# A fused attention and low-rank mixer kernel on one core: the fifth batch's k and q turned in two halves around the first mixer's u, casts moved by some heads, and the first batch's V placed later

## The chip, the cores and the metric

The kernel runs on one core of one Trainium2 chip. A core has TensorE (PE: matmuls and transposes into PSUM banks), VectorE (DVE), ScalarE (ACT), GpSimd (POOL) and SyncE (SP), each with a queue of its own that is worked off in order, and 16 DMA engines that all queues share. The metric is the device time of one execution in microseconds; the median of several runs is given. "Before" is the kernel without the change.

## The reference

Eight batches of eight heads, 576 tokens, head width 64, model width 512, inner width 2048:

```python
scores = scale * np.matmul(q, k.transpose(0, 1, 3, 2))
cum = np.cumsum(np.maximum(s, 0.0), axis=-1)
bias = -(cum[:, :, :, None] - cum[:, :, None, :])
scores = np.where(causal, -1000000000.0, scores + np.minimum(bias, 0.0))
attn = softmax(scores)
x = (attn @ v).transpose(0, 2, 1, 3).reshape(B, S, H * D)
u = x + (x.transpose(0, 2, 1) @ U @ V).transpose(0, 2, 1)
out = u + np.maximum(u @ w_ch1, 0.0) @ w_ch2
```

U is 576 x 32, V 32 x 576, `w_ch1` 512 x 2048 and `w_ch2` 2048 x 512. All are float32; the kernel multiplies in bfloat16.

## The kernel before, in words

**Groups.** The batches go in four groups of two (`GROUPS`). For a group the attention of both batches fills `x_sb`, `mix(g)` adds the low-rank part and so makes u in place, u is transposed into `uT`, and two layers follow: `layer1` (L542, matmuls at L551, ReLU on ScalarE at L558 into `hT`) and `layer2` (L561, matmuls at L570, sum on VectorE at L581, output by SyncE at L584 or L589). `beside` (L595) writes the instructions of a group's layers and of the next group's attention alternately, by estimated costs. That order is fixed when the program is built: each engine then runs its own instructions in the order in which they were written, and waits where it must. The buffers are `uT` one, `x_sb` two, the float32 stage of v `vf0` one, outputs `o` five, PSUM banks "s" three, "f" three, "pv" two.

**Attention of one head** (`scores`, L317; `weigh`, L361). Four score quanta, each into one "s" bank, each followed by an exponential on ScalarE (L329) into a tile `pT`; after the second quantum GpSimd masks the diagonal blocks (`affine_select`, L344). `weigh` multiplies with V (15 matmuls at L373), and VectorE divides by the sums (L379, L385). In the attentions from batch 2 on (`attention`, L404) a head's `weigh` comes behind the second quantum of the next head. After a head's quanta `at_head(h)` is called, and writes the loads that are to come at that place. In the code the head is `h` and the batch `c`; "(4, 2)" is batch 4, head 2.

**k and q.** Scores need k and q with the head's width along the partitions. Two heads are one pair, and a ring of eight pairs (`kT`, `qT`) holds two batches. The first three batches are loaded by `load_six` (a DMA issued by GpSimd, L164) and turned on TensorE: `turn_six` (L285) has six transposes at L296 into a PSUM bank, and two copies at L288, on VectorE or ScalarE. From batch 3 on it takes two steps. `cast(b)` (L153) issues two DMAs on GpSimd's queue, k and then q, that copy a batch from float32 to bfloat16 in DRAM (`kq_rows`). `turn_batch` (L766) then goes to SyncE's queue: for each pair a transposing DMA for k and one for q (`turn_kq`, L174), and for each pair two small DMAs with the bias rows (`bias_rows`, L281), which must follow the transposes of their pair. A transposing DMA waits for its cast; the queue waits with it.

**v.** `fetch_v` (L192, SyncE) loads a tile of float32 v into `vf0`, and `cast_v` (L198, GpSimd, copy at L200) makes bfloat16 of it in `v_raw`. `vf0` is overwritten only after its cast. `v_raw` also holds a column of ones beside each head, and zeros in half of the fifth tile (L693, L694 for the first batch).

**u.** `mix(g)` for g > 0: nine matmuls with U (L444), then for each of the nine token tiles one matmul with V (L518), an addition on VectorE (L522) and a transposing DMA on SyncE into `uT` (L526). `layer1` of group g starts with the first three tiles (`THIRDS`).

**The first batch** (`first_attention`, L678) has no layers beside it. `place_U` and `place_V` put U and V as bfloat16 into `U_cat` and `V_cat`; V goes to two blocks of rows, one copied by ScalarE and one by GpSimd (L146). The dictionary `turns` says behind which (head, quantum) which pair's k (0) or q (1) is turned, and into which PSUM bank; `weighed` says behind which quantum a finished head is weighed. `fill` writes matmuls on zeros (L315).

**Where the calls stand on SyncE's queue.** Before the change, from batch 3 on: V of batch 4 (behind batch 2's last head), `turn_batch(4)` with all four pairs, outputs of group 0, u of group 1 with the outputs between, then at (4, 0) batch 5's first two pairs, V of batch 5 and its other two pairs.

Of the kernel before, what the change touches and what calls it, by code (L numbers as in the profile page):

```python
# [22 lines left out]
TAIL = 4  # L23
# [18 lines left out]
def kernel(  # L42
# [12 lines left out]
    nc = tc.nc  # L55
    B, H, S, D = q.shape
# [7 lines left out]
    HP = H // 2  # L64
# [6 lines left out]
    def bank(tag, bufs):  # L71
        return psum.tile([128, 512], FP32, tag=tag, bufs=bufs, name="ps_" + tag)
# [5 lines left out]
    v_raw = [t.rearrange("p (t h e) -> p t h e", h=H, e=D + 1) for t in v_flat]  # L78
# [25 lines left out]
    def clear(ap, value=0.0, engine=None):  # L104
        pair = 0.0 if value == 0.0 else 1.0019378662109375
        (engine or nc.vector).memset(ap.bitcast(FP32), pair)  # L106
# [28 lines left out]
    def place_U(bi, copy=nc.gpsimd.tensor_copy):  # L135
        r, h = slice(R * bi, R * bi + R), slice(64 * bi, 64 * bi + 64)
        copy(U_cat[:, 5 * bi : 5 * bi + 4, r], U_f[:, :4])
        copy(U_cat[h, TAIL, r], U_f[h, 4])

    def place_V(bi, copies=(nc.gpsimd.tensor_copy, nc.gpsimd.tensor_copy)):  # L140

        for copy, r0 in zip(copies, (R * bi, 64 + R * bi)):
            rows = slice(r0, r0 + R)
            V_rows = V_cat[rows].rearrange("r t c -> r (t c)")
            if bi == 0:
                copy(V_rows[:, :S], V_f[rows])  # L146
            else:
                copy(V_rows[:, 640:], V_f[rows, :512])
                copy(V_rows[:, 576:640], V_f[rows, 512:])
# [3 lines left out]
    def cast(b):  # L153
        for i, src in enumerate((k, q)):
            nc.gpsimd.dma_start(
                out=kq[i, HP * b : HP * b + HP, :PAIR].rearrange("n (r c) -> r n c", r=128),
                in_=src[b]
                .rearrange("(n h) s d -> n (h s d)", h=2)
                .rearrange("n (r c) -> r n c", r=128),
            )  # L160

    def load_six(b, i, h0, h1):
        hs = slice(h0, h1)
        nc.gpsimd.dma_start(  # L164
            out=six[min(b, 1)][i][:, hs, :].rearrange("p h (s d) -> p h s d", d=D),
            in_=(k, q)[i][b, hs].rearrange("h (p s) d -> p h s d", s=SUB),
        )
# [14 lines left out]
    def v_rows(t):  # L182
        return slice(64, 128) if t == 4 else slice(0, 128)
# [8 lines left out]
    def fetch_v(b, t):  # L192
        rows = slice(128 * t, min(128 * t + 128, S))
        nc.sync.dma_start(
            out=vf0[v_rows(t), t], in_=v[b, :, rows].rearrange("h p d -> p h d")
        )

    def cast_v(b, t, engine=None):  # L198
        n = v_rows(t)
        (engine or nc.gpsimd).tensor_copy(v_raw[b // 2 % 2][n, 5 * (b % 2) + t, :, :D], vf0[n, t])  # L200
# [76 lines left out]
    def bias_rows(n):  # L277
        if not n < BH // 2:
            return
        for to, r in ((kT, A_K), (qT, A_Q)):  # L280
            nc.sync.dma_start(out=to[n % RING][D:KA, : 2 * S], in_=aug_v[r, n])  # L281
# [3 lines left out]
    def turn_six(b, hp, which, scalar=0, tag="pv"):  # L285
        engines = [nc.scalar.copy if e < scalar else nc.vector.tensor_copy for e in range(2)]
        for one in turned(b, hp, which, tag, [(slice(0, 2), engines)]):
            one()  # L288
# [24 lines left out]
    def fill(ps, w):  # L313

        nc.tensor.matmul(ps[:, :w], lhsT=zero[:, :128], rhs=zero[:, :w], start=True, stop=True)  # L315
# [82 lines left out]
    def next_p():  # L398
        n_p[0] += 1
        if n_p[0] <= 2 * H:  # L400
            return first_p[(n_p[0] - 1) % H]
        return pT[(n_p[0] - 1) % len(pT)]
# [249 lines left out]
    clear(qT[3][D:, : 2 * S], 1.0, nc.gpsimd)  # L652
    for i in range(2):
        load_six(0, i, 6, 8)
    ps = bank("s", 3)
    for _ in range(6):
        fill(ps, 512)
# [20 lines left out]
    def first_attention():  # L678
        turn_six(0, 0, 0)
        turn_six(0, 0, 1, scalar=2)  # L680
        place_U(0, nc.scalar.copy)
        place_V(0, (nc.scalar.copy, nc.gpsimd.tensor_copy))
        ps = bank("s", 3)
        for _ in range(3):
            fill(ps, 512)
        turn_six(0, 1, 0, tag="f")
        for _ in range(2):
            fill(ps, 512)
        turn_six(0, 1, 1, tag="f")
        fill(ps, 512)  # L690
        for p in first_p:
            nc.vector.memset(p[:, PAD:D4], 1.0)
        nc.vector.memset(v_raw[0][:, :, :, D : D + 1], 1.0)  # L693
        nc.vector.memset(v_raw[0][:64, TAIL], 0.0)  # L694
        clear(zeros, 0.0)

        nc.sync.dma_start(
            out=kA[1][D : D + 1].rearrange("r n (h s) -> r (n h) s", h=2), in_=ones[:H]
        )
        for r in range(1, AUG):  # L700
            nc.sync.dma_start(
                out=qA[1][D + r : D + r + 1].rearrange("r n (h s) -> r (n h) s", h=2), in_=ones[:H]
            )
        for r in range(AUG):
            direct_rows(1, 0, HP, r)
        load_UV(1)
        nc.sync.dma_start(out=kq[:, :, PAIR:].rearrange("i n c -> (i n) c"), in_=zeros)
        nc.sync.dma_start(
            out=aug[1:4].rearrange("r n s -> n r s"),
            in_=ones.unsqueeze(1).to_broadcast([BH, 3, S]),  # L710
        )


        turns = {
            (2, 0): (2, 0, "f"), (2, 3): (2, 1, "pv"), (3, 2): (3, 0, "pv"), (4, 1): (3, 1, "f")
        }
        weighed = {(5, 1): 1, (5, 3): 1, (6, 1): 1, (6, 3): 1, (7, 1): 1, (7, 3): 1}
        halves = [mix_first(dt) for dt in (0, 2)]
        done = []
        for h in range(H):  # L720
            p = next_p()
            fills = 0 if h < 2 or h > HP else 320 if h < HP else 448
            for n, _ in enumerate(scores(h // 2, h % 2, p, fills=fills)):
                if (h, n) in turns:
                    hp, which, tag = turns[h, n]
                    turn_six(0, hp, which, tag=tag)
                for _ in range(weighed.get((h, n), 0)):
                    weigh(*done.pop(0))
            done.append((0, h, p))
            for t in {1: (4, 0), 2: (1, 2), 3: (3,)}.get(h, ()):  # L730
                cast_v(0, t)
            if h in (3, 4):
                load_six(1, h - 3, 0, HP)
            if h == 5:
                load_w1(0)
        load_six(1, 0, HP, H)
        load_w1(1)
        load_six(1, 1, HP, H)
        for j in (2, 3):
            load_w1(j)  # L740

        one, two = halves
        next(one)
        weigh(*done.pop(0))
        next(one)
        next(one)
        weigh(*done.pop(0))

        nc.vector.memset(v_raw[0][:64, TAIL + 5], 0.0)
        for _ in one:  # L750
            pass
        next(two)
        on_scalar, on_vector = [nc.scalar.copy] * 2, [nc.vector.tensor_copy] * 2
        heads = slice(0, 1), slice(1, 2)
        k_copies = turned(
            1, 0, 0, "s", [(heads[0], on_scalar), (heads[1], on_vector)]
        )
        for copy in k_copies[:2]:
            copy()
        for _ in two:  # L760
            pass
        q_copies = turned(1, 0, 1, "s", [(hs, on_vector) for hs in heads])
        for copy in q_copies[:2] + k_copies[2:] + q_copies[2:]:
            copy()

    def turn_batch(b, p0=0, p1=HP):  # L766
        for n in range(HP * b + p0, HP * b + p1):
            turn_kq(n)
            if n > HP * b:
                bias_rows(n - 1)  # L770
        if p1 == HP:
            bias_rows(n)

    def second_at_head(h):
        if h == 0:
# [56 lines left out]
    def ahead_of(c):  # L832


        def at_head(h):

            if h == 0 and c == 3:
                turn_batch(c + 1)
            if h == 0 and c in (4, 6):
                cast(c + 1)  # L840
                turn_batch(c + 1, 0, 2)
                for t in range(5):
                    fetch_v(c + 1, t)
                turn_batch(c + 1, 2, HP)
            if h == 0 and c == 5:
                cast(c + 1)
                turn_batch(c + 1)
            if h == 6 and c == 2:
                cast(c + 2)
            if 5 <= h and c + 1 < B:  # L850
                for t in ((0,), (1, 2), (3, 4))[h - 5]:
                    cast_v(c + 1, t)
            if h == 7 and c in (2, 4):
                for t in range(5):
                    fetch_v(c + 2, t)

        return at_head
# [52 lines left out]
```

## Time and profile before

| what | value |
|---|---|
| median of 3 runs | 373.87 us (373.39 to 374.41) |
| the profiled execution | 374.12 us, span from first to last instruction 372.4 us |
| mean granted clock of TensorE | 1.000 |
| DMA | 124039 packets, 49.32 MB |
| first scores of batch 1 / 2 / 3 / 4 / 5 / 6 | 30.2 / 78.7 / 101.1 / 137.5 / 167.2 / 222.3 us |
| first layer of groups 1, 2, 3 begins | 137.2 / 221.9 / 306.7 us |

The profile names an instruction by line, engine and what it writes and reads ("kT<-kq_rows"). In a timeline the first column is the start in microseconds from the span's start, the second the duration, and "xN" says how many alike were merged; what stands in brackets is the engine's idle time before, and what ended it. SPq rows are issues on SyncE's queue, and their durations hold the time for which the queue waited. The DMA itself lands later. The trace also has marks of these landings; where a landing is told with its time, it is the last mark that the DMA's semaphore got. In the DMA view q1 is the queue of SyncE's and ScalarE's DMAs, and q0 that of GpSimd's.

### The profile page before, as it was taken

What the parts mean: (1) busy time and instruction counts of PE and PEld (TensorE: products, weight loads), DVE (VectorE), ACT (ScalarE), POOL (GpSimd) and SP (SyncE); (2) the same over time, 40 slices, a digit from 0 to 9 for tenths busy, and PEclk for the clock granted to TensorE, in tenths of its full rate; (3) what the DMA queues carried; (4) which work ended last, traced back from release to release, by engine and by line L of the source; (5) the groups of instructions that cost most, each with busy time, mean ns of one, the idle gap of its engine ahead of it and who ended that gap; (6) DMA issues with size and microseconds to landing.
All of it is one profiled execution on the core that took longest, in us unless ns stands there. A gap on an engine that the chain in (4) does not pass through costs nothing.

```text
span 372.4 us, 8251 instructions
## 1 busy us (share of the span) xinstructions
PE 360.5 (97%) x3234; PEld 221.4 (59%) x3255; DVE 139.1 (37%) x310; ACT 212.3 (57%) x499; POOL 108.3 (29%) x166
## 2 busy tenths in 40 slices
PE   7899999999999989999999999999999999999996
PEld 3577684568776446666654446666654446565444
DVE  8878855652224551221243721212233710000221
ACT  6988982479897019889850009888840007772000
POOL 8895982312634103243150003242120000000000
PEclk9999999999999999999999999999999999999999
DMA  7999999798799869999995558892001550000122
GB/s 118 181 153 213 173 207 214 153 204 164 138 242 178 104 157 172 180 212 163 217 155 165 101 141 154 156 193 47 2 30 58 126 143 28 2 0 30 70 72 85
DMA packets 124039, 49.32 MB, mean 132 GB/s; under 512 B 104896, under 2 KB 119200, under 8 KB 124000
## 3 DMA queue, kind: packets, MB, share of 16 engines
q1 hardware_dynamic: 104374, 34.45, 45.6%
q0 software_dynamic: 19056, 14.22, 27.7%
q8 instruction: 25, 0.41, 0.5%
q10 hardware_dynamic: 570, 0.12, 0.2%
q14 instruction: 14, 0.11, 0.1%
HBM read 37.67 MB, written 15.79 MB: 144 GB/s over the span
## 4 chain that ended last, share of the span: by engine, by line
PE 87%; DVE 6%; ACT 3%; issue 1%; POOL 1%; DMA 1%; ACTq 0%; POOLq 0%; DVEq 0%
PE ps_f L551 32%; PE ps_f L570 31%; PE ps_s L323 11%; PE ps_pv L373 8%; DVE x_sb L522 2%; ACT pT L329 1%; PE ps_f L518 1%; PE ps_f L444 1%; PE ps_pv L296 1%; DVE qT L288 1%; DVE kT L288 1%; PE ps_s L315 1%; ACT x_sb L329 1%; DMA uT<-x_sb 1%; ACT hT L558 1%
## 5 line engine op out<-in xcount | busy, mean ns | idle before, releaser
L551 PE MATMUL ps_f<-uT,w 128*128 128x384 bf16 (+3 forms) x832 | 158.4, 313 | 0.9 <-DMA uT<-x_sb 0.9
L329 ACT ACTIVATE pT<-ps_s 128x448 bf16<-128x448 f32 x232 | 109.8, 526 | 60.4 <-PE ps_s L323 58.6
L570 PE MATMUL ps_f<-w,hT 128*128 128x512 bf16 (+1 forms) x571 | 136.8, 373 | 1.1
L558 ACT ACTIVATE hT<-ps_f 128x384 bf16<-128x384 f32 (+3 forms) x208 | 101.9, 492 | 46.8 <-PE ps_f L551 45.5
L551 PEld LDWEIGHTS <-w 128*128 128x128 bf16 x832 | 72.3, 98 | 34.0 <-issue 2.2
L570 PEld LDWEIGHTS <-hT 128*128 128x128 bf16 x592 | 54.9, 98 | 57.1 <-issue 3.9
L344 POOL TENSOR_SCALAR_AFFINE_SELECT pT<-pT 128x640 bf16<-128x640 bf16 x58 | 43.9, 756 | 150.5 <-ACT pT L329 150.0
L323 PE MATMUL ps_s<-qT,kT 68*128 68x128 bf16 (+9 forms) x576 | 80.8, 239 | 3.2 <-ACT pT L329 0.8
L323 PEld LDWEIGHTS <-kT 68*128 68x128 bf16 (+1 forms) x576 | 46.2, 97 | 29.9 <-issue 5.5
L379 DVE RECIPROCAL rec<-ps_pv 128x5 f32<-128x5 f32 x64 | 12.5, 195 | 120.2 <-PE ps_pv L373 119.9
L581 DVE TENSOR_TENSOR o<-x_sb,ps_f 128x512 f32<-128x512 bf16 (+1 forms) x37 | 24.9, 673 | 86.3 <-PE ps_f L570 85.6
L373 PEld LDWEIGHTS <-pT 128*128 128x128 bf16 x870 | 33.7, 97 | 8.7 <-ACT pT L329 1.0
L373 PE MATMUL ps_pv<-v_raw,pT 128*128 128x65 bf16 x870 | 36.7, 194 | 0.7 <-POOL pT L344 0.5
L385 DVE TENSOR_TENSOR x_sb<-ps_pv,rec 128x320 bf16<-128x320 f32 (+1 forms) x64 | 29.3, 458 | 2.3
L200 POOL CAST v_raw<-vf 128x512 bf16<-128x512 f32 (+1 forms) x35 | 21.3, 616 | 16.3 <-DMA vf<-in_v_dram 11.4
L522 DVE TENSOR_TENSOR x_sb<-x_sb,ps_f 128x512 bf16<-128x512 bf16 x32 | 21.2, 687 | 7.4 <-PE ps_f L518 7.1
L288 DVE COPY kT<-ps_pv 64x576 bf16<-64x576 bf16 x14 | 11.2, 803 | 3.5 <-ACT kT L288 2.8
L296 PEld LDWEIGHTS <-hT 96*128 96x128 bf16 x144 | 8.1, 97 | 4.4 <-DMA hT<-in_k_dram 1.1
L518 PE MATMUL ps_f<-ux_sb,V_cat 128*128 128x512 bf16 x27 | 10.2, 379 | 0.4
L288 DVE COPY qT<-ps_pv 64x576 bf16<-64x576 bf16 x12 | 9.6, 803 | 2.5 <-ACT qT L288 1.8
L315 PE MATMUL ps_s<-uT 128*128 128x512 bf16 (+2 forms) x21 | 7.6, 451 | 1.8 <-DVE uT L106 1.6
L288 ACT COPY kT<-ps_pv 64x576 bf16<-64x576 bf16 x4 | 3.2, 796 | 9.2 <-PE ps_pv L296 9.2
(109 smaller groups left out, 152.0 us busy)
## 6 DMA issues: line engine op xcount, KB each, us to landing
out_dram<-o SPq DMA_DIRECT2D x31, 256.0 KB
vf<-in_v_dram SPq DMA_DIRECT2D x28, 256.0 KB
w<-in_moe_w_ch_dram POOLq DMA_DIRECT2D x8, 512.0 KB, 9.4
kq_rows<-in_k_dram POOLq DMA_DIRECT2D x5, 576.0 KB, 7.0
kq_rows<-in_q_dram POOLq DMA_DIRECT2D x5, 576.0 KB, 10.0
out_dram<-o SPq DMA_DIRECT2D x10, 128.0 KB
hT<-in_k_dram POOLq DMA_DIRECT2D x4, 288.0 KB, 8.6
hT<-in_q_dram POOLq DMA_DIRECT2D x4, 288.0 KB, 10.6
```

The lines of the kernel that those rows point to most:

```text
L200: (engine or nc.gpsimd).tensor_copy(v_raw[b // 2 % 2][n, 5 * (b % 2) + t, :, :D], vf0[n, t])
L288: one()
L323: nc.tensor.matmul(ps[:, col : col + w], lhsT=kt_[:rows, c + kc : c + kc + 128], rhs=qt_[:rows, c + qc : c + qc + w], start=True, stop=True,)
L329: nc.scalar.activation(p[:, at : at + w], ps[:, :w], EXP, scale=scale)
L344: nc.gpsimd.affine_select(out=diagonal, in_=diagonal, compare_op=ALU.is_ge, fill=0.0, base=0, pattern=[[0, 5], [1, 128]], channel_multipli ...
L373: nc.tensor.matmul(pv3[:, it, :], lhsT=p[:, at : at + 128], rhs=vr[:, 5 * bi + j, h, :], start=(j == 0), stop=(j == it),)
L385: nc.vector.tensor_mul(x[:, 5 * bi : 5 * bi + n, h * D : h * D + D], pv3[:, :n, :D], rec[:, :n].unsqueeze(2).to_broadcast([128, n, D]),)
L522: nc.vector.tensor_add(x[:, t, :], x[:, t, :], hp_)
L551: nc.tensor.matmul(f1[:, :cw], lhsT=w1[:, kt, 128 * nf : 128 * nf + 128], rhs=uT[:, kt, c0:c1], start=(kt == 0), stop=(kt == 3),)
L558: nc.scalar.activation(hT[:, nf, c0:c1], f1[:, :cw], RELU)
L570: nc.tensor.matmul(f2[:, :cw], lhsT=hT[:, kt, 128 * t : 128 * t + 128], rhs=w2[:, kt, cs], start=(kt == 0), stop=(kt == 15 and not more),)
L581: nc.vector.tensor_add(o[:, :cw], x_sb[g % 2][:, t, cs], f2[:, :cw])
```

## The change

In the first batch V is placed behind heads 3 (ScalarE's half) and 4 (GpSimd's half) instead of ahead of head 0; the ones and zeros in `v_raw` are written by GpSimd ahead of the attention instead of by VectorE; the third pair's k is turned behind (1, 2) instead of (2, 0), the fourth pair's k behind (3, 3) instead of (3, 2); the first weighing comes one quantum later; and the k of batch 1's first half is loaded a head sooner, ahead of the third cast of v.

From batch 2 on: `cast(4)` moves from (2, 6) to (2, 5). `turn_batch(4)` at (3, 0) does the first two pairs only, and the other two follow at (4, 0), so behind `mix(1)` on SyncE's queue. `cast(5)` and all of `turn_batch(5)` move from (4, 0) to (4, 2), V of batch 5 from there to (3, 7). `cast(6)` and `turn_batch(6)` move from (5, 0) to (5, 5). Batch 7 stays as it was. `turn_batch` writes the last bias rows at the end of each call.

```diff
@@ def place_V
         for copy, r0 in zip(copies, (R * bi, 64 + R * bi)):
+            if copy is None:
+                continue
...
     for i in range(2):
         load_six(0, i, 6, 8)
+    nc.gpsimd.memset(v_raw[0][:, :, :, D : D + 1], 1.0)
+    nc.gpsimd.memset(v_raw[0][:64, TAIL], 0.0)
...
         place_U(0, nc.scalar.copy)
-        place_V(0, (nc.scalar.copy, nc.gpsimd.tensor_copy))
...
-        nc.vector.memset(v_raw[0][:, :, :, D : D + 1], 1.0)
-        nc.vector.memset(v_raw[0][:64, TAIL], 0.0)
...
         turns = {
-            (2, 0): (2, 0, "f"), (2, 3): (2, 1, "pv"), (3, 2): (3, 0, "pv"), (4, 1): (3, 1, "f")
+            (1, 2): (2, 0, "f"), (2, 3): (2, 1, "pv"), (3, 3): (3, 0, "pv"), (4, 1): (3, 1, "f")
         }
-        weighed = {(5, 1): 1, (5, 3): 1, (6, 1): 1, (6, 3): 1, (7, 1): 1, (7, 3): 1}
+        weighed = {(5, 2): 1, (5, 3): 1, (6, 1): 1, (6, 3): 1, (7, 1): 1, (7, 3): 1}
...
-            for t in {1: (4, 0), 2: (1, 2), 3: (3,)}.get(h, ()):
+            if h == 3:
+                place_V(0, (nc.scalar.copy, None))
+            for t in {1: (4, 0), 2: (1,), 3: (3,)}.get(h, ()):
                 cast_v(0, t)
-            if h in (3, 4):
-                load_six(1, h - 3, 0, HP)
+            if h == 2:
+                load_six(1, 0, 0, HP)
+                cast_v(0, 2)
+            if h == 4:
+                load_six(1, 1, 0, HP)
+                place_V(0, (None, nc.gpsimd.tensor_copy))
...
     def turn_batch(b, p0=0, p1=HP):
         for n in range(HP * b + p0, HP * b + p1):
             turn_kq(n)
-            if n > HP * b:
+            if n > HP * b + p0:
                 bias_rows(n - 1)
-        if p1 == HP:
-            bias_rows(n)
+        bias_rows(n)
...
@@ def at_head
-            if h == 0 and c == 3:
-                turn_batch(c + 1)
-            if h == 0 and c in (4, 6):
-                cast(c + 1)
-                turn_batch(c + 1, 0, 2)
-                for t in range(5):
-                    fetch_v(c + 1, t)
-                turn_batch(c + 1, 2, HP)
-            if h == 0 and c == 5:
+            if (c, h) == (2, 5):
+                cast(4)
+            if (c, h) == (3, 0):
+                turn_batch(4, 0, 2)
+            if (c, h) == (4, 0):
+                turn_batch(4, 2, HP)
+            if (c, h) in ((4, 2), (5, 5)):
                 cast(c + 1)
                 turn_batch(c + 1)
-            if h == 6 and c == 2:
-                cast(c + 2)
+            if (c, h) == (6, 0):
+                cast(7)
+                turn_batch(7, 0, 2)
+                for t in range(5):
+                    fetch_v(7, t)
+                turn_batch(7, 2, HP)
...
-            if h == 7 and c in (2, 4):
+            if h == 7 and c in (2, 3, 4):
                 for t in range(5):
                     fetch_v(c + 2, t)
```

## The prediction

> **What bounds the kernel now.** First the page's busy shares and its chain of the work that ended last; then TensorE's waits from 30 us on; then the queues around the two places that the diff touches.
>
> ```profile
> PE 360.5 (97%) x3234; PEld 221.4 (59%) x3255; DVE 139.1 (37%) x310; ACT 212.3 (57%) x499; POOL 108.3 (29%) x166
> ...
> PE 87%; DVE 6%; ACT 3%; issue 1%; POOL 1%; DMA 1%; ACTq 0%; POOLq 0%; DVEq 0%
> ```
>
> TensorE is the bound. It runs its instructions in the order they were written and nothing takes work off it, so every microsecond in which it waits is a microsecond of the result. The waits of TensorE from 30 us to the end (us in total, times, longest) are few:
>
> ```profile
> PE ps_f L551 <- DMA uT<-x_sb: 0.9, 1, 0.9
> PE ps_pv L373 <- POOL pT L344: 0.5, 1, 0.5
> PE ps_s L323 <- ACT x_sb L329: 0.5, 2, 0.3
> ```
>
> So behind the first attention at most some 2 us can be won, and any new wait is paid in full. The rest of the idle time lies in the first 20 us, where ScalarE shows the pace (its timeline, with the idle time before a piece in brackets):
>
> ```profile
> 8.90 0.67 ACT L146 CAST V_cat<-w 32x576 bf16<-32x576 f32 x1
> 9.59 6.45 ACT L329 ACTIVATE pT<-ps_s 128x448 bf16<-128x448 f32 x16
> 16.70 1.69 ACT L329 ACTIVATE pT<-ps_s 128x448 bf16<-128x448 f32 x4 [0.66 <-PE ps_s L323]
> 18.25 1.76 ACT L329 ACTIVATE x_sb<-ps_s 128x448 bf16<-128x448 f32 x4
> 20.31 1.74 ACT L329 ACTIVATE x_sb<-ps_s 128x448 bf16<-128x448 f32 x4 [0.30 <-PE ps_s L323]
> ```
>
> **Part 1, the first batch.** V's ScalarE copy (0.67 us) leaves 8.90 and goes behind head 3's exponentials. The first scores run at 9.05 to 9.4, so head 0 can begin at most 0.2 us sooner. The copy then falls into the 0.66 us in which ScalarE waits at 16.04 for head 4's scores; these waited for VectorE's copies of the third pair (12.99 to 16.25, two of 1.61 us). VectorE loses the memsets of L693 and L694 (0.12 and 0.28 us) and gets the third pair's k two score quanta sooner, so its chain starts at about 11.8 instead of 12.99 and head 4's scores can start at about 15.5 instead of 16.30. With the copy in between, ScalarE reaches head 4 at about 16.5, 0.2 us sooner. TensorE's head 6 waited until 19.92 for the last copy of q (17.94 + 1.64); that now ends near 18.8, and what ends last is TensorE's own row of scores and two weighings (0.45 us each), near 19.55: 0.37 us sooner. From there TensorE is packed to 28.8. I take **-0.4 us**. Bounds: -0.8 (the 0.66 and 0.30 gaps both vanish, less what the front cannot give) to +0.5: GpSimd gets the memsets (the like ones at L806 and L808 took 0.46 and 0.53 us), the k load of batch 1 goes ahead of the third V cast, and the first weighing, now a quantum later, needs all five casts (the last ran 17.96 to 18.57).
>
> **Part 2, batch 4's cast one head sooner.** GpSimd's two cast issues (0.74 us each, 96.50 to 97.95) and two V casts stood ahead of head 7's mask, at 99.08; TensorE's weighing waited for that mask 0.49 us. With the casts behind head 5 (mask 93.17 to 93.92) the mask can start near 98.4. I take **-0.5 us**; 0 to -0.5. The transposes of batch 3 that the cast now meets are needed only at 111 and 116 (heads 4 and 6 of batch 3), and the SP queue that they hold up carries nothing due before 114.
>
> **Part 3, the halves around u.** SyncE's queue and TensorE's first layer of group 1:
>
> ```profile
> 129.20 0.24 SPq L281 DMA_DIRECT2D qT<-aug_rows  x1
> 129.54 1.18 SPq L584 DMA_DIRECT2D out_dram<-o  x2
> 130.76 1.08 SPq L589 DMA_DIRECT2D out_dram<-o  x2
> 131.93 6.53 SPq L526 DMA_TRANSPOSE uT<-x_sb  x5
> 138.56 0.53 SPq L589 DMA_DIRECT2D out_dram<-o  x1
> 139.15 5.67 SPq L526 DMA_TRANSPOSE uT<-x_sb  x4
> 144.91 0.53 SPq L589 DMA_DIRECT2D out_dram<-o  x1
> ```
>
> VectorE has the first tile of u ready at 128.49 + 0.69 = 129.2, but the queue reaches it at 131.93, behind batch 4's last transposes and four outputs. With only two pairs ahead, the queue is free in time (batch 5's V loads, now in this place, are issued by about 124: the last V cast that they wait for ends at 122.7, and an issue takes about 1 us). So u's transposes start 2.7 us sooner, the third lands near 134.4 instead of 137.06, and the wait of 0.89 us at 137.19 goes: **-0.9 us** (0 to -0.9).
>
> Now the half that was moved behind. Nine transposes of u at 1.31 us apart and two outputs of 0.55 hold the queue from 129.2 to about 142.2. Then come two k and two q transposes (1.35 us apart, from 113.15 to 117.56 in the trace) and the bias rows of the third pair (0.43 and 0.27): the last of them is issued at about 148.4. In before, such bias rows land with the transposes ahead of them, about 2.1 us after their issue (118.35 to 120.48). That is 150.5 at best. TensorE needs this pair at head 4 of batch 4:
>
> ```profile
> 150.80 0.36 PE L323 MATMUL ps_s<-qT,kT 68*128 68x64 bf16 x4
> ```
>
> less the 0.89 us: 149.9. So even undisturbed it is 0.6 us late. And it is disturbed. Batch 5's cast follows head 2's mask on GpSimd; the mask ran at 145.29, so the cast is issued at 145.29 + 0.70 - 0.89 = 145.1. What a cast does to the SP queue's small packets is seen in the DMA view of before, cast issued at 140.63, in the stretches 143 to 146 and, without a cast, 157 to 159:
>
> ```profile
> q0 software_dynamic: 454, 0.52, 109.5%
> q1 hardware_dynamic: 32, 0.00, 1.5%
> ```
>
> ```profile
> q1 hardware_dynamic: 1854, 0.47, 105.0%
> ```
>
> The columns are packets, MB and share: q1 falls from 900 packets a microsecond to 10, and in 146 to 150 it gets 522, about 130 a microsecond. The landing marks agree: the transpose of u issued at 141.77, 1.1 us behind that cast, landed at 151.50, 10.9 us behind it; its neighbour issued at 140.46 landed at 145.81; with the cast of 169.86, bias rows issued at 172.24 landed at 177.15. A q transpose issued at 146.2, also 1.1 us behind its cast, lands by the first of these at 145.1 + 10.9 = 156.0, and the bias rows, which are queued behind it, at about 156.3. TensorE stands at head 4 from 149.9: **+6.4 us**. Bounds: +0.6 (no starving) to +7.3 (a q transpose of this kind has 1152 packets of 256 B against 512 of u's).
>
> **Part 4, what such a stall does to the clock.** The first fills of the trace, 512 columns each:
>
> ```profile
> 1.64 2.74 PE L315 MATMUL ps_s<-uT 128*128 128x512 bf16 x6 [1.64 <-DVE uT L106]
> ...
> 6.36 0.81 PE L315 MATMUL ps_s<-uT 128*128 128x512 bf16 x3
> ```
>
> Six span 2.74 us, 0.42 apart; three later ones 0.21 apart. TensorE that has been idle runs at half speed, here until the fills of 4.37 to 5.14, still 0.38 apart: some 3.4 us, 1.7 us lost. No row shows a warm TensorE idle for 6 us, so the price is 0 to 1.7; I take **+1.7**, the only row there is of a start from idle. The Trainium skill states this as a rule ("TensorE: Matmul & The Clock Gate", Part 1: The HAM clock gate): after an idle window of about 3.4 us the clock is halved and full again only after a busy one; by that page the loss is half of 3.4, 1.7 us, for a wait over one such window, and nothing for a shorter one. The start of the trace agrees with the second half of this; no row of before shows the first.
>
> **The other moves cost nothing as long as their cover holds.** Batch 6's cast, now at head 5 of batch 5, is issued near 186.7; by the last one's times (6.8 and 10.3 us to landing) its eight transposes fill the queue from 193.5 to about 210, u's first three of group 2 end at about 215.7 and land near 217. TensorE needs them at 221.9: 5 us of cover. If it were gone, the wait would be what u is late. Outputs are held back until 210 too; the sixth then waits for its buffer under 1 us on VectorE, while TensorE has another bank. Batch 5's transposes, begun near 157, are needed 4 us later than before and have 3 us to spare.
>
> **Sum** against the profiled execution (372.4 span, 374.12 with what lies around it): -0.4 - 0.5 - 0.9 + 6.4 + 1.7 = **+6.3 us**. The median of the runs is 0.25 below the profiled one, so 373.87 + 6.3 = **380.2 us**.
>
> **Rivals.**
> - *The cast does not starve the queue where it counts* (0.11): the pair lands at 150.5 to 151.5. Then -1.8 + 0.6 to 1.6, no cold clock: 372.7 to 373.7. For it: the u transpose issued at 140.46 still got through 2.7 us late only. Against it: two big transposes are behind that point, not one small.
> - *The pair is there in time, not slower but faster* (0.11): the queue frees u's transposes sooner or head 4 comes later by over 0.6 us, so only the three gains stay: 372.1 us. It decides at 149.9: both transposes and both bias transfers of the pair must have landed by then. Against it: nine issues of 1.31 us are in the trace, and u cannot be ready before 129.2.
> - *The stall without the cold clock* (0.22): 378.5 us. The stall with it (0.52): 380.2 us.
> - *The late outputs or the first batch's casts cost 1 to 2 us besides, or instead* (0.04): slower by 1.2 or more.
>
> **Numbers.** With runs of this kernel 0.3% is 1.1 us. Faster by more: the second rival and a third of the first, 0.15. Within: the rest of the first, 0.07. Slower: 0.78. The two stall cases alone go from 377 (a stall of 5 us, warm) to 382.5 (7.3 us, cold, no gain in part 1). They hold 0.74, with some of that outside these ends, so eight in ten needs most of the first rival and part of the second: the range reaches down to 372.3.
>
> **What would show it.** Right: a wait of TensorE of 5 to 7 us at L323, the first scores of head 4 of batch 4, released by a DMA into kT or qT, near 149; fills or matmuls behind it at half pace; the 0.89 at L551 and the 0.49 at L373 gone; ScalarE's 0.66 filled by V's copy. Wrong: no wait there, the bias rows of that pair landed before 150, or q1 keeping several hundred packets a microsecond beside the cast.

## The result, and the profile after

The changed kernel takes **386.86 us** in the median of five runs (386.11 to 387.31) against 373.87 of the kernel before (five runs, 373.39 to 374.96): a ratio of 1.034, with an interval of 1.032 to 1.036. It is 13.0 us slower; forecast was 6.3 us, with an upper end of 382.5. The ratios given here and below leave out runs more than 1.5% above the fastest of their kernel, and are not the ratios of the medians beside them. The profiled execution has 386.68 us and a span of 385.0, 12.6 more than the span before.

The line numbers of after are two higher than those of before in the functions told of here (L323 is now L325, L551 is L553). From the page of after, the busy time, the granted clock in 40 slices and the chain that ended last:

```profile
PE 362.9 (94%) x3234; PEld 223.0 (58%) x3255; DVE 138.8 (36%) x308; ACT 212.1 (55%) x499; POOL 108.7 (28%) x168
...
PEclk9999999999999999599999999999999999999999
...
PE 84%; DVE 4%; issue 3%; ACT 3%; DMA 2%; SPq 1%; POOL 1%; POOLq 0%; ACTq 0%; DVEq 0%
```

TensorE is busy for 2.4 us more with as many instructions, and its clock is half in one slice; the other 10 us are idle time. TensorE's waits from 28 us on name them, and those ahead of 28 us show a new one in the first batch (us in total, times, longest):

```profile
PE ps_s L325 <- DMA qT<-aug_rows: 9.3, 1, 9.3
PE ps_pv L375 <- POOL pT L346: 2.1, 1, 2.1
```

```profile
PE ps_s L325 <- DMA kT<-parts: 0.9, 1, 0.9
```

The wait for u (0.9 at L551) and that for batch 2's last mask (0.5 at L373) are gone, as forecast. The 9.3 us lie where they were expected, at the first scores of head 4 of batch 4, and what is behind them runs at half pace (TensorE's timeline; compare two L553 matmuls at 159.59 and at 165.57):

```profile
159.27 0.53 PE L325 MATMUL ps_s<-qT,kT 68*128 68x64 bf16 x4 [9.31 <-DMA qT<-aug_rows]
159.59 0.85 PE L553 MATMUL ps_f<-uT,w 128*128 128x384 bf16 x2
...
165.57 0.49 PE L553 MATMUL ps_f<-uT,w 128*128 128x384 bf16 x2
```

Busy time by stretches of the same trace shows the same: from 150 to 152.5 TensorE has nothing, and from 152.5 to 163.5 its mean clock is 0.53 (the column before the last two):

```profile
150.00:152.50 2.50, 0.00 (x0) 0.00 (x0) 0.00 (x0) 0.49 (x2) 0.00 (x0) 1.00 1.19 195
152.50:163.50 11.00, 4.23 (x31) 2.84 (x32) 0.69 (x2) 2.01 (x4) 0.75 (x1) 0.53 0.96 152
```

Following the start of each head's first scores through both traces gives the account, where "step" is how much the delay grows or shrinks at that place, against the head before it:

| first scores of | before | after | step | forecast |
|---|---|---|---|---|
| batch 1, head 0 (part 1) | 30.22 | 30.60 | +0.38 | -0.4 |
| batch 3, head 0 (part 2) | 101.09 | 101.14 | -0.32 | -0.5 |
| batch 4, head 0 (part 3) | 137.52 | 136.51 | -1.05 | -0.9 |
| batch 4, head 4 (the wait) | 150.80 | 159.27 | +9.47 | +6.4 |
| batch 4, head 5 (the clock) | 154.24 | 164.53 | +1.83 | +1.7 |
| batch 7, head 0 (the mask wait) | 251.95 | 264.53 | +2.29 | 0 |
| sum | | | +12.6 | +6.3 |

**The stall.** SyncE's queue, answering to the rows shown of before:

```profile
142.32 2.19 SPq L176 DMA_TRANSPOSE kT<-kq_rows  x1
144.61 1.26 SPq L176 DMA_TRANSPOSE qT<-kq_rows  x1
145.96 2.43 SPq L176 DMA_TRANSPOSE kT<-kq_rows  x1
148.49 5.60 SPq L176 DMA_TRANSPOSE qT<-kq_rows  x1
154.18 0.43 SPq L283 DMA_DIRECT2D kT<-aug_rows  x1
154.71 0.26 SPq L283 DMA_DIRECT2D qT<-aug_rows  x1
```

The first two are the third pair's: their packets are through the DMA engines by 147.4, as the cast's begin (the q part's last landing mark is at 150.24, when TensorE had waited 0.3 us). The next two are the fourth pair's, and only behind them stand the third pair's bias rows. Batch 5's cast is issued by GpSimd at 145.24 and 145.98. From 147 on its packets take the engines, SyncE cannot issue the last transpose (5.60 us instead of 1.3), and the bias rows are issued at 154.71 and land at 159.02; 0.25 us later TensorE goes on. The DMA view of 148 to 151 has the same two lines as before had in 143 to 146 (packets, MB, share):

```profile
q0 software_dynamic: 459, 0.52, 108.4%
q1 hardware_dynamic: 120, 0.02, 6.9%
```

**The third wait.** Batch 6's cast and turn, moved to head 5 of batch 5, hold SyncE's queue until 219.4. Behind them come outputs, u of group 2, again outputs, and then batch 7's first two pairs and its V:

```profile
219.53 1.84 SPq L591 DMA_DIRECT2D out_dram<-o  x4
221.47 4.55 SPq L528 DMA_TRANSPOSE uT<-x_sb  x3
...
235.90 2.09 SPq L591 DMA_DIRECT2D out_dram<-o  x3
244.26 1.31 SPq L176 DMA_TRANSPOSE kT<-kq_rows  x1
...
255.78 4.11 SPq L196 DMA_DIRECT2D vf<-in_v_dram  x5
```

u's first three began at 204.79 before. TensorE does not wait for u here. But batch 7's cast now meets these outputs; its q part landed at 247.96 (234.58 before), and the first tile of V, behind the first two pairs, at 259.02 (243.21 before). TensorE itself is 10.3 us behind by then, so against it u is 6.4 us later, the cast 3.1 and V 5.5. On GpSimd the cast of V stands ahead of the mask:

```profile
259.07 0.61 POOL L202 CAST v_raw<-vf 128x512 bf16<-128x512 f32 x1 [6.81 <-DMA vf<-in_v_dram]
259.63 0.75 POOL L346 TENSOR_SCALAR_AFFINE_SELECT pT<-pT 128x640 bf16<-128x640 bf16 x1
```

TensorE waits 2.11 us for that mask.

**The first batch.** ScalarE's gap ahead of head 4 is filled by V's copy, as forecast, and head 4 starts 0.79 us sooner. Head 6 then waits (the timeline's idle time at 20.74):

```profile
15.78 0.66 ACT L148 CAST V_cat<-w 32x576 bf16<-32x576 f32 x1
16.34 1.65 ACT L331 ACTIVATE pT<-ps_s 128x448 bf16<-128x448 f32 x4
17.89 1.64 ACT L331 ACTIVATE x_sb<-ps_s 128x448 bf16<-128x448 f32 x4
20.74 1.42 ACT L331 ACTIVATE x_sb<-ps_s 128x448 bf16<-128x448 f32 x3 [1.20 <-PE ps_s L325]
```

### The profile page after: what moved, and what is told of

Its sections match the earlier page's. It is cut to its first block, busy times and chain, and to the rows that moved or that the text cites. A ratio compares the mean times of both kernels' runs of the same rounds, so it can differ in the third digit from the quotient of the medians.

```text
span 385.0 us, 8253 instructions
## 1 busy us (share of the span) xinstructions
PE 362.9 (94%) x3234; PEld 223.0 (58%) x3255; DVE 138.8 (36%) x308; ACT 212.1 (55%) x499; POOL 108.7 (28%) x168
## 4 chain that ended last, share of the span: by engine, by line
PE 84%; DVE 4%; issue 3%; ACT 3%; DMA 2%; SPq 1%; POOL 1%; POOLq 0%; ACTq 0%; DVEq 0%
PE ps_f L572 30%; PE ps_f L553 30%; PE ps_s L325 10%; PE ps_pv L375 8%; DVE x_sb L524 2%; PE ps_f L520 2%; ACT pT L331 1%; DMA qT<-aug_rows 1%; PE ps_f L446 1%; PE ps_s L317 1%; DMA kT<-parts 1%; PE ps_pv L298 1%; SPq L176 1%; DVE kT L290 1%; ACT x_sb L331 1%
## 5 line engine op out<-in xcount | busy, mean ns | idle before, releaser
L553 PE MATMUL ps_f<-uT,w 128*128 128x384 bf16 (+3 forms) x832 | 159.6, 315 | 0.0
L325 PE MATMUL ps_s<-qT,kT 68*128 68x128 bf16 (+9 forms) x576 | 81.5, 240 | 12.7 <-DMA qT<-aug_rows 9.3
L553 PEld LDWEIGHTS <-w 128*128 128x128 bf16 x832 | 72.8, 98 | 33.2 <-issue 1.3
L325 PEld LDWEIGHTS <-kT 68*128 68x128 bf16 (+1 forms) x576 | 46.3, 97 | 40.0 <-issue 15.9
L290 DVE COPY kT<-ps_pv 64x576 bf16<-64x576 bf16 x14 | 11.2, 804 | 3.6 <-ACT kT L290 2.8
L331 ACT ACTIVATE x_sb<-ps_s 128x448 bf16<-128x448 f32 (+1 forms) x16 | 7.8, 666 | 1.2 <-PE ps_s L325 1.2
```

What stands on the lines that cost most here:

```text
L325: nc.tensor.matmul(ps[:, col : col + w], lhsT=kt_[:rows, c + kc : c + kc + 128], rhs=qt_[:rows, c + qc : c + qc + w], start=True, stop=True,)
L331: nc.scalar.activation(p[:, at : at + w], ps[:, :w], EXP, scale=scale)
L553: nc.tensor.matmul(f1[:, :cw], lhsT=w1[:, kt, 128 * nf : 128 * nf + 128], rhs=uT[:, kt, c0:c1], start=(kt == 0), stop=(kt == 3),)
```

## The experiments

The kernel before was run beside each series on the same chip, with a median of 373.8 to 374.0 us. The first six are the changed kernel with one thing put back or moved.

**1. Batch 4 turned whole again.** `turn_batch(4)` at (3, 0); all else as in the change.

```diff
-                turn_batch(4, 0, 2)
-            if (c, h) == (4, 0):
-                turn_batch(4, 2, HP)
+                turn_batch(4)
```

> The changed kernel with batch 4 turned whole at (3, 0), as before; everything else stays changed. Theory (the half behind u is late, and the cast of batch 5 starves it): TensorE's wait of 9.3 us at head 4 of batch 4 and the 10.2 us at half clock go, together 11.3 us; batch 5's V loads now stand behind all of batch 4's transposes, so u may come late: a wait of 0 to 2 us at the first layer of group 1. Time 375 to 378 us. Rival (the wait comes from elsewhere, for instance from batch 5's V loads): the wait at head 4 stays, time over 383 us.

Two runs, 378.85 and 381.37 us; the profile is of the second. The wait at head 4 is gone, so the halves make it. But the time is above what was expected, since u is late:

```profile
PE ps_f L553 <- DMA uT<-x_sb: 3.5, 1, 3.5
```

```profile
129.30 4.67 SPq L196 DMA_DIRECT2D vf<-in_v_dram  x5
134.06 0.57 SPq L591 DMA_DIRECT2D out_dram<-o  x1
134.72 6.51 SPq L528 DMA_TRANSPOSE uT<-x_sb  x5
```

V of batch 5, which the change moved ahead of u, now comes behind the whole turn, and u's transposes start at 134.72 instead of 129.26. The wait of 3.5 us brought half clock for 6.83 us. So V's new place needs the halves; the halves with V at its old place were not run.

**2. Batch 5's cast alone ahead of u.** `cast(5)` at (3, 5), its turn still at (4, 2).

```diff
-            if (c, h) in ((4, 2), (5, 5)):
-                cast(c + 1)
-                turn_batch(c + 1)
+            if (c, h) == (3, 5):
+                cast(5)
+            if (c, h) == (4, 2):
+                turn_batch(5)
```

(and batch 6 at (5, 5) as in the change)

> The changed kernel with the cast of batch 5 issued at (3, 5), so that it has landed before u is turned; batch 5's transposes stay at (4, 2) and batch 4's second half at (4, 0). Theory (starvation by the cast makes the wait long): the pair's bias rows land near 150.5, TensorE waits 0.3 to 1.5 us at head 4 instead of 9.3, and the clock stays at 1.0: time 375 to 378 us. Rival (the length of SyncE's queue alone, nine u's and two outputs ahead, makes the wait): the wait stays at 5 us or more, time over 381 us.

Two runs, 380.64 and 381.76 us; the wait at head 4 is 2.6 instead of 9.3:

```profile
PE ps_s L325 <- DMA qT<-aug_rows: 2.6, 1, 2.6
```

```profile
148.49 1.39 SPq L176 DMA_TRANSPOSE qT<-kq_rows  x1
149.97 0.43 SPq L283 DMA_DIRECT2D kT<-aug_rows  x1
```

The same transpose, issued at the same time as in the changed kernel, takes 1.39 us to issue with no cast beside it, and 5.60 with one. The cast is worth 6.7 of the 9.3 us. The other 2.6 are the queue, and not more: here V's loads met the cast and u began 1.85 us later than in the changed kernel. The time falls less than the wait, because the half clock stayed (6.83 us from 152.13; head 5 of batch 4 comes 2.99 us late by it).

**3. Batch 5's cast and turn one head later**, at (4, 3) instead of (4, 2).

> The changed kernel with the cast of batch 5 and its transposes at (4, 3) instead of (4, 2). Theory: the cast is issued near 148.9 instead of 145.2, its packets begin near 150.3, when the transposes of the third pair are through, so TensorE waits 0.6 to 2 us at head 4 and the clock stays at 1.0; batch 5's first pair is still in time: time 375 to 379 us. Rival (queue length alone): the wait stays at 5 us or more, time over 381 us.

Two runs, 376.93 and 385.40 us; the profile is of the first. There the wait is 1.8 us, the clock stays whole, and the wait for the mask of batch 6 is 1.3:

```profile
PE ps_s L325 <- DMA qT<-aug_rows: 1.8, 1, 1.8
```

One head on GpSimd, 4.2 us (the cast is issued at 149.40 instead of 145.24), decides over some 7 us of stall. What the second run met was not seen; its mean clock of 0.987 is that of the changed kernel.

**4. Batch 6's cast and turn back at (5, 0).**

```diff
-            if (c, h) in ((4, 2), (5, 5)):
+            if (c, h) in ((4, 2), (5, 0)):
```

> The changed kernel with the cast of batch 6 and its transposes at (5, 0) instead of (5, 5). Theory (the later cast 6 holds back the outputs and u of group 2, these meet the cast of batch 7, V of batch 7 lands late, and GpSimd stands in a V cast ahead of a mask): TensorE's wait of 2.1 us for the mask at batch 6 goes, time 384 to 385 us. Rival (the wait at batch 6 follows from the stall at batch 4 or from the V loads at (3, 7)): it stays, time 386 to 387 us.

Two runs, 384.24 and 385.70 us, some 1.9 us below the changed kernel. The wait for the mask in batch 6 is gone. GpSimd's rows at the place of the 6.81 us:

```profile
254.54 0.61 POOL L202 CAST v_raw<-vf 128x512 bf16<-128x512 f32 x1 [2.46 <-DMA vf<-in_v_dram]
255.10 0.75 POOL L346 TENSOR_SCALAR_AFFINE_SELECT pT<-pT 128x640 bf16<-128x640 bf16 x1
```

That shows the cause of the third wait. The wait at head 4 was 8.8.

**5. The first batch with batch 1's k load back behind head 3.**

```diff
-            for t in {1: (4, 0), 2: (1,), 3: (3,)}.get(h, ()):
+            for t in {1: (4, 0), 2: (1, 2), 3: (3,)}.get(h, ()):
...
-            if h == 2:
+            if h == 3:
                 load_six(1, 0, 0, HP)
-                cast_v(0, 2)
```

> The changed kernel with batch 1's first k load back behind the third head's casts of V (behind head 3), as before; the rest of the first batch stays changed. Theory (the earlier k load holds up the bias rows of the fourth pair, which TensorE awaits at head 6 of the first batch): TensorE's 0.9 us wait for a DMA into kT there goes, head 6 starts near 19.5 to 19.7 instead of 20.35, and batch 1 starts 0.2 to 0.5 us sooner than in the kernel before instead of 0.4 us later. Rival (the moved first weighing or V's copy costs it): head 6 stays near 20.3.

One run, 387.3 us. The early load is what head 6 waited for: the wait for kT is gone, and head 6 starts at 19.33, 0.59 us sooner than before. Yet batch 1 starts 1.6 us later than before:

```profile
PE ps_f L553 <- DMA w<-in_moe_w_ch_dram: 1.7, 1, 1.7
```

The first part of w1 landed at 30.36, having been just in time before (28.71, first used at 28.80). With this order the DMAs of the first 30 us give back at w1 what is won at head 6.

**6. Three pairs ahead of u and one behind it.** `turn_batch(4, 0, 3)` and `turn_batch(4, 3, HP)`.

> The changed kernel with three pairs of batch 4 turned ahead of u, at (3, 0), and only the fourth behind it, at (4, 0). Theory: the third pair is there long before head 4, so the 9.3 us wait and the half clock go; u is not later, since SyncE's queue was idle from 119.4 to 122.2 in the changed kernel; the fourth pair, behind u and half in the cast's way, lands between 148 and 157 and is needed at 157: a wait of 0 to 2 us at head 6. Time 375 to 378 us. Rival (u comes late again): 1 to 4 us at the first layer of group 1.

Two runs, 380.67 and 383.92 us; the profile is of the second. No wait at head 4, but one for u of 4.8 us and half clock for 6.83 us: u's transposes start at 135.93, 6.7 us later than in the changed kernel. The theory's gap in SyncE's queue was not there; the rival holds. But the two transposes more ahead of V's loads are the smaller part of it, since batch 4's turn already begins late:

```profile
94.89 1.70 SPq L176 DMA_TRANSPOSE qT<-kq_rows  x1
...
106.67 0.24 SPq L283 DMA_DIRECT2D qT<-aug_rows  x1
...
114.57 2.06 SPq L176 DMA_TRANSPOSE kT<-kq_rows  x1
```

Batch 4's cast was issued at 94.30. Batch 3's last transpose, 0.6 us behind it, landed at 106.65; its bias rows waited for that, and the queue with them, so the turn begins 5.7 us later than in the changed kernel (114.57 instead of 108.90), where that transpose was issued 3.4 us ahead of the cast. What the order of three and one costs by itself is therefore not shown.

**7. The three-and-one order with the causes of 3, 4 and 5 mended**: casts 5 and 6 at (4, 3) and (5, 0), the k load back.

> All that the runs point to: three pairs ahead of u and one behind, batch 5's cast and transposes at (4, 3), batch 6's at (5, 0) as before, batch 1's k load as before. Theory: no wait of over 0.6 us is left behind 30 us, the u wait of 0.9 and the mask wait of 0.5 of the kernel before are gone, the first batch gains 0.2 to 0.5: 371.8 to 373.0 us, so 0.3 to 0.5% faster than before. Rival (the later cast of batch 5 makes its first pair late, or the fourth pair of batch 4 is late): 374 us or more.

Twelve runs, median 377.09 us (373.90 to 383.41), ratio 1.0055 (1.0029 to 1.008). The profiled one (379.48) waits 2.8 us for u, 1.4 for w1 and 1.1 at head 4 of batch 5. It has the collision of 6 too: batch 3's last transpose was issued 0.8 us behind batch 4's cast and landed at 105.55, and batch 4's turn begins 3.1 us later than in the changed kernel. The fastest of the twelve, 373.90, is at the median of the kernel before.

**8. The kernel before from batch 2 on, with batch 4's cast at (2, 5), and the first batch as in 5.**

> The kernel before from batch 2 on, but batch 4's cast at (2, 5), and the changed first batch with the k load as before; batch 4 is turned whole at (3, 0) and batches 5 and 6 are cast and turned as before. Theory: the mask wait of 0.5 at batch 2 shrinks to 0.2, the first batch gains 0.2 to 0.5, the u wait of 0.9 stays: 373.0 to 373.5 us. Rival (the earlier cast costs as much elsewhere): 373.9 us or more.

Ten runs, median 375.14 us (373.84 to 381.38), ratio 1.0038 (1.0015 to 1.006). Batch 3 gains 0.32 us and batch 4 another 1.05, as in the changed kernel but with nothing halved. Waits of 2.6 us for w1 in the first layer cost more than that. They also make TensorE reach u 2.2 us later, while u's transposes begin at 132.01 (131.93 before), so the 1.05 us here say nothing on the cast.

**9. The kernel before with batch 4's cast at (2, 5) alone.**

```diff
-            if h == 6 and c == 2:
+            if h == 5 and c == 2:
```

> The kernel before with one call moved: batch 4's cast behind head 5 of batch 2 instead of head 6; nothing is halved and no other cast moves. Theory (the gains of the change come from this cast alone): the wait of 0.5 us for batch 3's first mask and the wait of 0.9 us for u of group 1 are both gone, since the eight transposes of batch 4 end sooner; batch 3 starts 0.32 us and batch 4 1.05 us sooner than before, no clock below 1.0, and the time is about 1.05 us below before: 372.8 us. Rival (the halves are needed for the gain at u): the u wait stays between 0.5 and 0.9 us, batch 4 starts only 0.3 to 0.5 us sooner: 373.4 to 373.6 us.

Twelve runs, median 374.22 us (372.76 to 378.52), ratio 1.0023 (0.9995 to 1.005). In the profiled execution (373.24) the theory's gains are there: batch 3 gains 0.32 us (the mask awaited before is batch 2's last), batch 4 another 1.05, and u's transposes begin at 129.44 instead of 131.93. So part 3's gain does not need the halves. But six of the runs are above 374.5, and the gain is not there in the median.

**10. The kernel before with the changed first batch alone.**

> The kernel before with the changed first batch alone, batch 1's k load a head sooner as in the change; from batch 2 on all is as before. Theory (the load of k holds up the fourth pair's bias rows, and the rest of the batch only gives back what it won): head 4 starts 0.7 to 0.8 us sooner than before, head 6 waits about 0.9 us for kT and starts 0.4 us later, batch 1 starts 0.3 to 0.5 us later; the time is 0.4 us above before: 374.3 us. The prediction's own term: head 6 0.4 us sooner, 373.5 us. Second rival (the first layer's w1 takes what is left, as with the k load put back): a wait for w1 at the first layer and batch 1 over 1 us later: 375 us or more.

Eleven runs, median 373.88 us against 373.76, ratio 0.9998 (0.9986 to 1.001). Head 6 waits 0.8 us for kT and batch 1 starts 0.8 us later. Then the wait for u is gone and batch 4 starts 0.26 us *sooner* than before: in this execution u landed when TensorE came. What the first batch loses, up to 0.9 us, is made good where the kernel before waits for u. Part of that is not explained: u's transposes also began 0.8 us sooner than before (131.11), and why is open.

**11. As 9, with GpSimd's casts of batch 5's V one head later**, to find the cause of the scatter in 9.

```diff
-                for t in ((0,), (1, 2), (3, 4))[h - 5]:
+                later_v = ((), (0, 1), (2, 3, 4))
+                for t in (later_v if c == 4 else ((0,), (1, 2), (3, 4)))[h - 5]:
```

> The kernel before with batch 4's cast behind head 5 of batch 2, and GpSimd's five casts of batch 5's V one head later (two behind head 6, three behind head 7 of batch 4). The same cast move alone had runs from 372.8 to 378.5 us, those above 374.6 with a mean clock of 0.991 to 0.998. Theory: in its trace GpSimd stood 3.8 us in the first of these V casts until V had landed at 160.12, and the mask of head 5 behind it ended 0.8 us before TensorE's weighing at 162.26, so a landing 3 us later makes TensorE wait some 2 us and halves its clock. With the V casts a head later the masks of heads 5 and 6 no longer stand behind that landing: the runs lie within 1.5 us, clock 1.0, median 372.5 to 373.2 us. Rival (the scatter comes from another place, for instance the cast's meeting with batch 3's last bias rows or u's transposes): the runs scatter as before, some above 376 us, median 373.5 to 374.5.

Twelve runs, median 373.47 us (372.86 to 378.39), ratio 1.0001 (0.9977 to 1.0024): the scatter stays, so this theory falls. But the profiled execution is one of the later ones (374.85), and it waits elsewhere:

```profile
PE ps_f L551 <- DMA uT<-x_sb: 1.6, 1, 1.6
```

```profile
95.27 2.00 SPq L174 DMA_TRANSPOSE qT<-kq_rows  x1
...
100.15 0.24 SPq L281 DMA_DIRECT2D kT<-aug_rows  x1
105.16 0.24 SPq L281 DMA_DIRECT2D qT<-aug_rows  x1
...
111.64 3.15 SPq L174 DMA_TRANSPOSE kT<-kq_rows  x1
...
132.65 6.53 SPq L526 DMA_TRANSPOSE uT<-x_sb  x5
```

Batch 4's cast was issued at 94.17; batch 3's last q transpose came 1.1 us behind it and landed at 105.14. In experiment 9 that transpose was issued at 93.52, ahead of the cast at 94.38, and landed at 96.59. Here the queue stands until 105.16, batch 4's turn starts 2.6 us later than in 9 and u 3.2 us later. It is the same collision as at head 4 and in the traces of 6 and 7, by 1.75 us on the queue.

**12. The kernel of 9 once more, beside 11.**

> The same kernel as the cast of batch 4 behind head 5 of batch 2 alone, once more beside the one with the V casts moved. Theory: again runs from 372.8 to some 378 us, about half of them above 374 with a clock below 1.0; if the profiled run is one of those, it shows TensorE waiting 2 to 3 us for the mask of head 5 or 6 of batch 4 (near 162 or 165 us), with the V cast ahead of it waiting for V, and half clock from there. Rival: a late profiled run shows its wait elsewhere; or all runs now lie within 1.5 us, and the scatter was of that one series.

Twelve runs, median 373.71 us (372.88 to 379.19), ratio 1.0 (0.998 to 1.002). Half of them lie within 0.6 us of 372.9; the profiled one (372.89) is one of these and has none of the waits. Of the six above 374 us only the slowest has a mean clock clearly below 1 (0.995), so the theory's half clock is not what most of them lose. The runs of 375 to 379 us were not caught in a trace, so whether the collision of 11 makes those too is open; that it can be as dear, 6 and 7 show. No version tried beats the kernel before by more than can be measured.

## Why the prediction was right in kind and wrong in size

**What bounds it, the place, the releaser, the direction**: as predicted. TensorE stands at L325, at the first scores of head 4 of batch 4, from 149.96 (forecast 149.9), for a DMA into qT, and the cast that does it was issued at 145.24 (forecast 145.1). Without the halves there is no such wait (experiment 1), and without the cast 2.6 us of it are left (experiment 2).

**The +6.4 us was mis-sized; it measured +9.47.** The failing step is "the last of them is issued at about 148.4", and with it that the bias rows land "at about 156.3". The third pair's first transpose was forecast at 142.2 and issued at 142.32, but its issue took 2.19 us and not 1.35, so the fourth pair's k, by the forecast's spacing due at 144.9, came at 145.96. With that two transposes stood behind the cast, not one: the fourth pair's k (145.96) and q (148.49), both ahead of the third pair's bias rows. (The first rival speaks of "two big transposes" behind that point; the sum counts one.) Both have 1152 packets by the prediction's own count. Of these 2304 none moved before 149.7 and 518 did by 154 (in the microseconds from 149 on 2, 93, 146, 138 and 139); the third pair's 2304 had taken from 144.5 to 147.4. The landing of 10.9 us behind a cast was taken from one transpose of u with 512 packets, and by the first of its marks (its last, at 151.82, is 11.2 us behind); here the two landed 12.1 and 13.1 us behind it, and the bias rows 13.8. The upper bound of +7.3 knew of the 1152 packets but counted one transpose, and the issue of 5.60 us, which delays the rows behind it, was in no term. By experiment 2, where u began 1.85 us later, the part of the cast is 6.7 us (forecast 5.8) and that of the undisturbed queue at most 2.6 (forecast 0.6).

The Trainium skill says that a DMA engine serves the queues that have work in turn, one packet of each ("DMA: Bandwidth & Descriptors", Queues, rings and completion order). From 150 to 154 the trace's counts fit that, if its packets are the page's: 516 of q1 beside 581 of q0. From 148 to 150 there are 27 beside 302, and 25 of the 27 are packets of four bytes. Whether q1 had more packets ready in that time the trace does not show, so it does not speak against the rule.

**The clock term was right**: +1.7 forecast, +1.83 measured. The half pace, taken from the start of the trace, came for a warm TensorE too, in a stretch of 10.24 us from 152.89 on, of which it worked the last 3.9. The rival without it is refuted. That the size came so close is partly luck: the same step is 1.42 and 1.43 us in experiments 4 and 5, behind waits of 8.8 and 7.8, and 2.99 in experiment 2, behind one of 2.6. The prediction's side remark that a wait shorter than one window costs nothing is refuted too, by experiments 2 and 7.

**"The other moves cost nothing as long as their cover holds" failed for batch 6's cast: +2.29 us.** The 5 us of cover for u was sized well enough that TensorE did not wait for u. What was late next was not followed: u and outputs held back on the queue until 238, batch 7's cast among them, V of batch 7 behind that cast, GpSimd's cast of V behind V, the mask behind that. Experiment 4 shows it. The rival of late outputs, "1 to 2 us besides", named the kind and was given 0.04.

**Part 1: -0.4 forecast, +0.38 measured.** Head 4 came as forecast: its scores start at 15.52 (forecast 15.5), and ScalarE reaches it at 16.34 (16.5). TensorE's work ahead of head 6 also ended where it was forecast, at 19.42 (19.55). The step that failed is that head 6 waits for nothing else than "TensorE's own row of scores and two weighings": it waited for the fourth pair's bias rows, which landed at 20.05 (18.65 before), because batch 1's k load was issued at 15.59 instead of 18.52, beside them. The bound of +0.5 had named this load. Experiment 5 confirms the load; in 10 the loss did not reach the time, since the wait for u was gone.

**Parts 2 and 3** came with -0.32 and -1.05 (forecast -0.5 and -0.9). But part 3's reason was only half of it: experiments 9 and 12 have the same 1.05 us with batch 4 turned whole, from the cast alone, as long as that cast misses batch 3's last transpose. Where it doesn't, that the queue "carries nothing due before 114" does not help: in the traces of 6, 7 and 11 the queue stood until 105 to 107, and batch 4's turn and u behind it were late by 2.6 to 5.7 us and 3.2 to 6.7 us (in 6 and 7 with two more transposes ahead of u).

The steps missed in size add up: 0.78 in part 1, 0.18 and -0.15 in parts 2 and 3, 3.07 in the wait, 0.13 in the clock and 2.29 in batch 7 are the 6.3 us between forecast and result.

## What to carry to other kernels

When a casting DMA on one queue can meet small-packet DMAs on another, count every packet that stands between the cast and the row that is awaited, in the order of issue, and not only the last one; in experiments 9 and 11 a shift of 1.75 us on the queue, from ahead of the cast to behind it, made one transpose land 8.6 us later. Follow a late queue to its end: the first engine may have cover, and the fourth one behind it may not. And small transfers that finish a buffer may be better directly behind their own transposes than behind the next pair's: here the data of the pair was there at 150.24 and its bias rows at 159.02. No run here tried that order, and it has a price: the queue stands until those transposes have landed, 2.4 us for the fourth pair's k here.

## What the runs showed of the hardware that was not expected

**Half clock comes in whole units, and after waits under one unit.** Away from the start and the end of the span every stretch at half clock is 3.41, 6.83 or 10.24 us long, that is one, two or three times 3.413. Waits of 9.3 us brought 10.24; of 8.8, 7.8, 4.8, 3.5 and 2.6 us 6.83; of 2.8 and 2.4 us 3.41; another of 2.4, and those of 2.1, 1.8 and below, none. What tells them apart is where the wait falls. In each trace all changes of the clock inside the span lie on steps of 3.413 us, counted from its first record of full clock. At full clock, half clock followed each of the eight steps in which TensorE waited for 1.97 us or more (1.97 in experiment 2) and none of those in which it waited for 1.73 us or less; the waits of 2.1 and 2.4 us that brought none lie across two steps, with 1.73 us as the larger part. So the stretch can begin in the wait (2.0 us behind its start in experiment 2) or after it (0.95 us behind its end in experiment 7), and the same wait costs more or less by where it falls. The Trainium skill has the unit but a longer least wait, an idle window of about 3.4 us ("TensorE: Matmul & The Clock Gate", Part 1: The HAM clock gate); these runs show half clock after 2.4 to 2.8 us.

**A backlog of small packets holds the issuing queue itself.** A transpose that SyncE issues in 1.3 us took 5.60 us behind a cast, and everything behind it on the queue moved by that.
